# Halo columns by a matmul with the shifted identity, and a new instruction order, in the backward pass of a gated long-convolution block

## The chip, the cores and the metric

The kernel runs on one core of a Trainium2 chip. The metric is device time in microseconds (us), the median of several runs. One further execution is recorded by the hardware profiler; all profile lines come from it.

## The reference

The forward function takes a sequence of S = 2048 rows of D = 512 bfloat16 channels. With `xn = layernorm(q)` it computes

```python
k_shift = sum(k_pad[:, t:t+S, :] * shift_k[:, 3 - t] for t in range(4))  # 4 taps along the rows
kv = k_shift * v
y  = irfft(rfft(kv, 2S) * rfft(ssm_k, 2S))[:S] + kv * ssm_D               # long convolution along the rows
s  = xn * y
g  = silu((sigmoid(xn @ w_gate) * (xn @ w_up)) @ w_down)                  # F = 1376 hidden columns
out = q + s * g
```

The kernel must return `out` and, by `jax.vjp` with a given `grad_out`, the gradients of q, k, v, shift_k, ssm_k, ssm_D, w_gate, w_up and w_down: ten outputs. The change is in the part that computes the gradients of k and shift_k. Since `k_shift` at row r reads k at rows r-3 to r, the gradient of k at row r is a sum of four products, of `d(k_shift)` at rows r to r+3 with the four taps. `d(k_shift)` is `d(kv) * v`.

## The kernel before

**Layout.** The 2048 rows are laid out as 128 partitions by NJ = 16 consecutive rows (row = 16 p + j). The 512 channels are cut into NG = 4 column groups of GW = 128. All buffers in the core's own memory are views of one slab, so every row of the profile says `slab`. The long convolution is a Fourier transform done in steps by matmuls on TensorE, with evacuations from PSUM (the memory that matmuls write) by ACT or DVE between them, products on DVE, and transposes.

**Stages.** Generator functions ("streams") run side by side: the gated layer forward and the layer norm (`strG`, `ln`), the forward convolution (`strK`, `strX`, `strV`), the backward pass of the gated layer (`strZ`, `strD`), the weight gradients (`dW`, 33 sums of matmuls over the rows), and the convolution backward (`frontC`, `backC`). `backC` is the last stage, together with what is left of `dW`. It loops over the four column groups `cg`. In each one it multiplies spectra, transforms back (`inv2`, `inv1`), which gives `dkv`, and then fills a tile `dks` of 16 + 3 columns of 128 channels: columns 0 to 15 are `dkv * vg`, and columns 16 to 18, the halo, are the columns 0 to 2 of the next partition, because the row after the last one of partition p is the first one of partition p + 1. The last partition has no successor, so the halo is zeroed first from partition 96 on. Two transfers by SyncE (SP) then copy partitions 1 to 112 and 113 to 127 down by one. The readers of the halo are the multiplications of lag 1, 2 and 3 at the end of the group, `dks[:, lag:lag + 16]` by a tap, which DVE adds up into the gradient of k. The matmuls between them (the gradient of ssm_k from `B2`, and `pa`, the gradient of the taps, which reads `dks[:, 0:16]` alone) do not read the halo. In the last group the multiplications run in two halves of 8 columns, and `last_rows` turns the sums for shift_k and ssm_D by small matmuls, which an evacuation and a small store each follow.

**How the order is set.** No instruction is issued where the program text stands. A recorder (`Rec.add`) numbers every operation (6158 of them) with its reads and writes, and `Rec.emit` issues them all from one line, L505, so every row of the profile shows that line. A dictionary `ORDER` holds one list of operation numbers per engine (tensor, vector, scalar, gpsimd, sync): the fixed queue of that engine. `60+2` stands for 60, 61, 62. A sixth list, `moves`, gives the common order in which transfers are issued, whichever engine issues them. `nc.evac(dst, src, n)` records a copy that either ACT or DVE can do; the list in which its number stands decides. `BANKS` holds one digit per PSUM tile, which picks its bank among those its kind may use. Engines wait for each other where data or a buffer asks for it, by semaphores that the framework adds; a wait holds up all that stands behind it in that engine's queue.

**Names used below.** At the start: ACT's operation 69 is a small load of ssm_D (L860); 194 (cg 0) and 468 (a later group) are SP's transposing loads of ssm_k (`ld_KT`, L823); 505 is a load of q; 79 is SP's load of most of w_down (L867); 250, 251 and 252 are ACT's copies of broadcast taps from PSUM (L887); 327 and 307 are ACT's activations of the gated layer's first blocks (L761); 62 is a sine table for the transform (L576) and 112 a second one (L618); 222 and 223 are DVE's layer norm statistics (L716); 262 is the first evacuation of the forward convolution (L903). At the end: 5765 and 5766 are the last group's halo operations, 5921 to 5924 are DVE's copies in `last_rows` (L1441) and 5838 its copy of the sums for ssm_D (L1410), 5925 to 5931 the small matmuls that read them, 5979 to 6002 the multiplications and additions of lags 1 to 3 in the second half (L1432, L1434); 6022 to 6156 are matmuls and evacuations of `dW`, whose last sums have 256 and 96 columns; 5982, 6021, 6089, 6123 and 6157 are stores of `dW` in ACT's queue (L1322), and 5977 and 6019 SP's stores of the gradient of k.

Of the kernel before, what the change touches and what calls it, by code (L numbers as in the profile page):

```python
# [16 lines left out]
P = 128  # L17
# [6 lines left out]
NJ = 16  # L24
# [3 lines left out]
GW = D // NG  # L28
# [47 lines left out]
    """,  # L76
    "vector": """
# [552 lines left out]
def kernel_impl(ctx, tc, A_q, A_k, A_v, A_shift_k, A_ssm_k, A_ssm_D, B_x, B_w_gate, B_w_up, B_w_down,  # L630
                grad_out, out_0, out_1, out_2, out_3, out_4, out_5, out_6, out_7, out_8, out_9):
    nc = tc.nc
# [22 lines left out]
    def ps(kind, shape, dt=f32):  # L655
        return nc.ps(kind, shape, dt)

    ident = Ring(ar, [P]).ap
# [704 lines left out]
    def backC():  # L1363
        for cg in range(NG):
# [26 lines left out]
            dks = dks_r.next()  # L1391
# [20 lines left out]
            for j in range(NJ):  # L1412
                for s in range(4):
                    nc.tensor.matmul(pa[32 * s:32 * s + 32], dks[:, j, 32 * s:32 * s + 32], kh[:, j:j + 4, 32 * s:32 * s + 32],
                                     start=(j == 0), stop=(j == NJ - 1))
# [110 lines left out]
```

## Time and profile before

| quantity | value |
|---|---|
| median of 3 runs | 452.25 us (451.94 to 456.33) |
| profiled execution | 453.04 us, of which the span is 450.9 us |
| TensorE matmul (PE) | 435.4 us busy, 97%, 4868 instructions |
| TensorE weight load (PEld, beside PE) | 305.6 us, 68% |
| VectorE (DVE) | 408.5 us, 91%, 626 instructions |
| ScalarE (ACT) | 281.4 us, 62%, 351 instructions |
| GpSimd (POOL) | 23.8 us, 5% |
| mean granted TensorE clock | 0.989 |
| transfers | 117.24 MB, mean 260 GB/s |

The span runs from the first to the last recorded instruction; what lies around it (start and end of the program) is in the time and not in the span. Busy times are of one engine each, and engines run side by side. In the page's slices each digit is a fortieth of the span (11.3 us) and gives tenths; a 9 stands for 90% or more. In the groups, a row gives the output and input tiles, their shape and type, the count, and behind the bar the busy time, the mean in ns, and the idle time of the engine just before these instructions with what ended most of it. In the timeline, a row gives start and length in us, the engine, and in brackets the idle time before it and what ended that. The engine names with q (ACTq, SPq) are the same engines' issue of transfers.

### The profile page before, as it was taken

Reading aid. Unit: us, or ns where it says so; the run is one execution under the profiler, and the core shown is the slowest. Engines: PE = TensorE matmul, PEld = TensorE weight load, DVE = VectorE, ACT = ScalarE, POOL = GpSimd, SP = SyncE. Lnnn points to the kernel's source line nnn. Section 1 sums busy time; section 2 is a strip of 40 time slices with the busy share of each in tenths; the row PEclk is TensorE's granted clock in tenths of the full one; section 3 lists DMA queues with packets and bytes.
Section 4 is the critical chain, followed back from the end, with each engine's and each line's share of the span. In section 5 each row is a group of like instructions: output and inputs, shape, how many; then the busy total and the mean of one; then the engine's idle time right before and its main releaser. Section 6 shows DMA issues by size and latency. Waiting matters only on the chain.

```text
span 450.9 us, 11537 instructions
## 1 busy us (share of the span) xinstructions
PE 435.4 (97%) x4868; PEld 305.6 (68%) x4903; DVE 408.5 (91%) x626; ACT 281.4 (62%) x351; POOL 23.8 (5%) x46
## 2 busy tenths in 40 slices
PE   8799999999999999999999999999999999999993
PEld 4586686867767677565656754444577888887883
DVE  8689999999987899999999987789799999999983
ACT  7578998898687586475844253337477456565431
POOL 8210310010100000000000000000000000000000
PEclk9889999999999999999999999999999999999998
DMA  7987989878859799999999999999999999999998
GB/s 242 338 313 167 319 248 339 246 211 237 297 166 302 210 244 227 263 346 298 332 247 318 287 254 266 279 206 235 243 242 176 290 243 267 208 274 228 248 277 267
DMA packets 196701, 117.24 MB, mean 260 GB/s; under 512 B 107510, under 2 KB 183338, under 8 KB 196522
## 3 DMA queue, kind: packets, MB, share of 16 engines
q1 hardware_dynamic: 187496, 111.88, 94.8%
q10 hardware_dynamic: 9154, 4.62, 3.5%
q8 instruction: 38, 0.62, 0.5%
q14 instruction: 13, 0.11, 0.1%
HBM read 43.87 MB, written 46.70 MB: 201 GB/s over the span
## 4 chain that ended last, share of the span: by engine, by line
PE 85%; DMA 7%; DVE 2%; ACT 2%; issue 1%; SPq 1%; ACTq 0%; DVEq 0%
PE psum L505 85%; DMA slab<-in_A_ssm_k_dram 3%; DVE slab L505 2%; ACT slab L505 2%; DMA out_dram<-slab 2%; DMA slab<-slab 1%; DMA slab<-KD 1%; SPq L505 1%; ACTq L505 0%; DVEq L505 0%
## 5 line engine op out<-in xcount | busy, mean ns | idle before, releaser
L505 PE MATMUL psum<-slab 128*128 128x256 bf16 (+5 forms) x4868 | 435.4, 300 | 9.0 <-ACT slab L505 3.3
L505 PEld LDWEIGHTS <-slab 128*128 128x128 bf16 (+2 forms) x4903 | 305.6, 96 | 138.7 <-issue 33.0
L505 ACT CAST slab<-psum 128x1024 bf16<-128x1024 f32 (+2 forms) x220 | 189.5, 903 | 128.4 <-PE psum L505 111.4
L505 DVE TENSOR_TENSOR slab<-slab 128x1024 bf16<-128x1024 bf16 (+4 forms) x302 | 240.0, 833 | 6.6 <-ACT slab L505 3.0
L505 DVE STREAM_TRANSPOSE slab<-slab 128x1024 f32<-128x1024 f32 x48 | 64.9, 1360 | 8.2 <-ACT slab L505 5.0
L505 ACT ACTIVATE slab<-slab 128x512 bf16<-128x512 bf16 (+5 forms) x63 | 53.1, 875 | 23.8 <-DVE slab L505 23.7
L505 DVE CAST slab<-psum 128x1024 bf16<-128x1024 f32 (+2 forms) x29 | 32.1, 1111 | 6.4 <-PE psum L505 6.2
L505 DVE TENSOR_TENSOR slab<-psum,slab 128x512 bf16<-128x512 f32 (+2 forms) x52 | 31.6, 610 | 6.6 <-ACT slab L505 5.2
L505 ACT ACTIVATE slab<-psum 128x512 bf16<-128x512 f32 (+1 forms) x48 | 27.5, 575 | 8.5 <-DMA slab<-in_A_ssm_k_dram 4.3
L505 POOL MEMSET slab<- 128x128 bf16 (+3 forms) x10 | 4.5, 449 | 268.9 <-DVE slab L505 162.3
L505 POOL TENSOR_TENSOR slab<-slab 128x2 f32<-128x2 f32 (+3 forms) x11 | 12.1, 1106 | 89.3 <-DVE slab L505 89.2
L505 DVE SCALAR_TENSOR_TENSOR slab<-slab 128x2 f32<-128x2 f32 (+2 forms) x41 | 14.4, 360 | 0.3
L505 ACT ACT_TABLE_LOAD x10 | 12.8, 1283 | 1.9 <-PEq L1510 1.7
L505 DVE SCALAR_TENSOR_TENSOR slab<-psum,slab 128x512 bf16<-128x512 f32 x16 | 10.7, 684 | 1.9 <-PE psum L505 1.8
L505 DVE BATCH_NORM_STATS2 slab<-slab 128x6 f32<-128x512 bf16 x16 | 10.6, 681 | 0.4 <-DMA slab<-in_A_q_dram 0.4
L505 DVE STREAM_SHUFFLE slab<-slab 128x1024 f32<-128x1024 f32 x8 | 10.6, 1322 | 0.0
L505 ACT COPY slab<-psum 128x1024 bf16<-128x1024 bf16 (+2 forms) x10 | 7.9, 802 | 2.8 <-PE psum L505 2.8
L505 DVE TENSOR_SCALAR slab<-slab 128x512 bf16<-128x512 bf16 (+6 forms) x26 | 6.7, 274 | 0.7 <-POOL slab L505 0.5
L505 DVE COPY slab<-psum 128x512 bf16<-128x512 bf16 (+1 forms) x9 | 4.2, 507 | 2.2 <-PE psum L505 2.2
L505 POOL TENSOR_SCALAR slab<-slab 128x1 f32<-128x1 f32 (+3 forms) x10 | 4.5, 450 | 0.5
L505 DVE MEMSET slab<- 32x192 uint32 (+3 forms) x10 | 1.5, 160 | 1.3 <-PEq L1510 0.9
L505 DVE BATCH_NORM_AGGREGATE slab<-slab 128x2 f32<-128x6 f32 x16 | 2.5, 166 | 0.0
(13 smaller groups left out, 9.0 us busy)
## 6 DMA issues: line engine op xcount, KB each, us to landing
slab<-KD SPq DMA_DIRECT2D x16, 512.0 KB, 4.8
hD<-slab SPq DMA_DIRECT2D x8, 704.0 KB, 7.2
duD<-slab SPq DMA_DIRECT2D x8, 704.0 KB, 5.1
dgD<-slab SPq DMA_DIRECT2D x8, 704.0 KB, 4.3
slab<-in_A_k_dram SPq DMA_DIRECT2D x4, 1024.0 KB, 7.5
KD<-slab SPq DMA_DIRECT2D x8, 512.0 KB, 6.2
VD<-slab SPq DMA_DIRECT2D x8, 512.0 KB, 6.5
out_dram<-slab SPq DMA_DIRECT2D x16, 256.0 KB, 4.2
```

The lines of the kernel that those rows point to most:

```text
L505: getattr(getattr(self.nc, eng), meth)(*[place(v) for v in a], **{x: place(v) for x, v in k.items()})
```

## The change

In `backC` the two halo transfers of each group become one matmul and one evacuation. The weights of the matmul are the columns 1 to 127 of the identity, so that output partition m takes input partition m + 1; its moving data are `dks[:, 0:3]`, 384 columns. The result, 127 partitions by 3 x 128 in PSUM (kind "x", one bank), is then copied to `dks[0:127, 16:19]`.

```diff
             nc.vector.memset(dks[96:P, NJ:NJ + 3, :], 0.0)
-            nc.sync.dma_start(dks[0:112, NJ:NJ + 3, :], dks[1:113, 0:3, :])
-            nc.sync.dma_start(dks[112:127, NJ:NJ + 3, :], dks[113:128, 0:3, :])
+            ph = ps("x", [3, GW])
+            nc.tensor.matmul(ph[0:P - 1], ident[:, 1:P], dks[:, 0:3, :], start=True, stop=True)
+            nc.evac(dks[0:P - 1, NJ:NJ + 3, :], ph[0:P - 1], 384)
             nc.vector.tensor_tensor(dkv, dkv, ksh, ALU.mult)
```

Two operations take the place of two, so all other numbers stay. The pairs are 3895/3896, 4520/4521, 5168/5169 and 5765/5766 for the four groups: the first is now a matmul, the second an evacuation, on DVE in the first and last group (3896, 5766) and on ACT in the two others (4521, 5169). SP's list and `moves` lose these eight numbers. `BANKS` grows from 349 to 353 digits, and many others of its digits differ.

All six lists are in a new order, over the whole kernel. The start of the lists of vector, scalar and sync, and the ends of the lists of tensor, vector and scalar (the diff of the whole lists has 260 lines):

```diff
 "vector"
-        5 93+1 54+1 6 95+2 58+1 35 31 36 32 37 64 33 41+1 39+1 165 175 53 48 166 222 138 137 140 139 141 262 143 328
-        144+1 318 111 308 280 290 223 401 151 114 203 113 345 193 224 542 367 225 281 226 253 587 497 136 309 687 329
+        5 93+2 6 58+1 35+1 54 96 37 31+2 64 41 97 42 39 55 40 165 48 53 175 137 166 138 140 139 141 222+1 262 328 143
+        145 144 318 111 308 290 156 224 113 280 225 401 151 203 345 193 542 367 253 587 794 226 281 228 136 309 497
 "scalar"
-        1 68 60+2 66 65 67 249+1 327 69 307 252 3 251 279 112 156 192 410 438 541 363 362 586 596 560 135 477 524 686
+        1 68 60+1 66 65 67 249+1 69 327 251+1 307 3 279 112 62 192 410 438 541 363 362 586 596 560 135 477 524 686 385
 "sync"
-        0 75 4 74 76+1 73 43 70 78 72 71 194 83 82 84 2 80 146 79 468 85 505 231 118 232 440 330 344 364 331 851 916
+        0 4 75 73 76 70 43 74 77+1 72 71 194 83 82 2 84 468 505 146 79 231 85 80 364 118 440 344 232 330+1 851 365 708
...
 "tensor", last lines
-        5947+8 5960+14 5991+2 5916+3 5994+1 6022+18 5975 5920 6041+5 5839+63 6047+2 5996+2 6003+8 5769+15 6012+6
-        6050+3 6056+14 5802+15 6071+16 6124 6090+5 6125 6096+25 5925+3 5931 6126+29
+        5839+63 6009+3 6056 5769+15 6035 6057 5975 6013+5 6036+4 5765 6058+1 6041 5802+15 6042+11 6060+19 5925+3 5931
+        6090+5 6080+7 6096+25 6124+31
 "vector", last lines
-        5307+1 5934 5369 5935 5242 5658 5903+1 5921 5956+3 5976 5978+2 5922 5999 5923 6000 5924 6001+1 5838 5929
+        5369 5763 5307 5767 5935 5308 5978 5934 5658 5956+1 5242 5958 5903 5959 5904 5921 5976 5922 5764 5766 5923
+        5979+1 5999+1 5924 6001 5838 6002 5929
 "scalar", last lines
-        5676 5532 5709 5744 5605 5819 5936 5820 5981 5785 6054 5982 5937 6055 5818 6020 6088+1 6021 5932 6122+1 6156+1
+        5656 5742 5709 5605 5532 5744 5676 5819 5936 5785 5820 5981 5937 5982 6020+1 5818 6054 5932 6055 6088 6122
+        6089 6123 6156+1
```

More of the change, by code (lines that the diff above doesn't have):

```diff
@@ L33 @@
     "tensor": """
[42 rows of a table removed]
[44 rows of a table added]
     """,
     "vector": """
[24 rows of a table removed]
[25 rows of a table added]
     """,
     "scalar": """
[16 rows of a table removed]
[17 rows of a table added]
     """,
     "gpsimd": """
-        87 56+1 29 98+1 30 63 38 34 100 92 116 88 86 89 91 101 90 103+1 115 105 107 142 81 108+2 106 227 117 501 102
-        912 935 1326 1657 1929 2261 3541 4743
+        56 87 57 90 29+1 63 38 34 91 86 98 88 99 115 89 100 116 101 103+2 108 81 109 107 142 106 92 110 102 227 117
+        501 1326 935 912 1657 1929 2261 3541 4743
     """,
     "sync": """
[11 rows of a table removed]
[10 rows of a table added]
     """,
     "moves": """
[13 rows of a table removed]
[12 rows of a table added]
     """,
@@ L154 @@
 BANKS = (
-    "32012111000113121000231010100010000101110000101000011101011001001001232011100001100001013101011012010011001011"
-    "00001111101020110101010100100101010001100110101001101001100122032132101010330101011010110102110100011210103110"
-    "01011322211212202002100210310300011231102301100022211202020213011022331131022101010200201301110020331110301210"
-    "3100101012201301201"
+    "32200102131110310001321010100010000101110000101000011101011001001001231011100001100001013101011002011011001001"
+    "00001110101131110101010100100101010001100110101001101001100131032103101012300101121012010131101201011210023110"
+    "01011322211212100102101010310101001123110230110002122120220021301110200311310221010102102013011101120331210301"
+    "21031001012112201301213"
 )
```

196 rows, old and new, of the table ORDER are left out of this document.

## The prediction

> **What bounds the kernel now.** I read the page first: the span, the busy shares, the granted clock by slices, the chain that ended last.
>
> ```profile
> span 450.9 us, 11537 instructions
> PE 435.4 (97%) x4868; PEld 305.6 (68%) x4903; DVE 408.5 (91%) x626; ACT 281.4 (62%) x351; POOL 23.8 (5%) x46
> PEclk9889999999999999999999999999999999999998
> PE 85%; DMA 7%; DVE 2%; ACT 2%; issue 1%; SPq 1%; ACTq 0%; DVEq 0%
> ```
>
> TensorE is busy for 97% of the span, and 85% of the last chain is matmuls. DVE, at 91%, is close behind. The second and third digit of the clock are 8s: TensorE lost clock somewhere in the first 34 us. Next, busy time by stretches, for the middle and for the start:
>
> ```profile
> 25.00:150.00 125.00, 124.27 (x1516) 92.17 (x1526) 118.41 (x158) 105.89 (x137) 10.20 (x9) 1.00 0.81 253
> 150.00:300.00 150.00, 149.11 (x1045) 90.75 (x1061) 137.70 (x278) 79.53 (x95) 0.94 (x2) 1.00 1.06 273
> 300.00:440.00 140.00, 138.50 (x2087) 105.69 (x2092) 131.60 (x138) 77.82 (x96) 0.73 (x1) 1.00 1.09 245
> ...
> 14.70:15.80 1.10, 1.08 (x10) 0.82 (x9) 0.96 (x2) 0.00 (x0) 0.49 (x2) 1.00 1.11 352
> 15.80:18.10 2.30, 0.00 (x0) 0.00 (x0) 0.41 (x1) 1.03 (x2) 0.00 (x0) 1.00 1.14 306
> 18.10:19.00 0.90, 0.00 (x0) 0.00 (x0) 0.28 (x1) 0.64 (x3) 0.00 (x0) 0.50 1.09 277
> 19.00:24.90 5.90, 5.86 (x40) 4.80 (x40) 3.05 (x6) 4.55 (x6) 0.00 (x0) 0.50 1.05 337
> 24.90:28.00 3.10, 3.05 (x35) 2.67 (x34) 2.92 (x5) 2.35 (x3) 0.00 (x0) 0.99 0.54 137
> ```
>
> Columns: stretch, length, busy time of PE, PEld, DVE, ACT and POOL, granted clock, DMA share, GB/s. From 25 to 440 us TensorE idles 0.73 + 0.89 + 1.50 = 3.1 us in all, so no order can win more than that there. At the start it stands still from 15.8 to 19.0, and its clock is at half from 18.1 to 24.9. The timeline of that place (start, length, engine) and the chain name the cause:
>
> ```profile
> 12.37 0.38 ACT L505 ACTIVATE slab<-psum 128x256 bf16<-128x256 f32 x1
> 16.62 0.39 ACTq L505 DMA_DIRECT2D slab<-in_A_ssm_D_dram  x1
> 17.07 0.60 ACT L505 ACTIVATE slab<-psum 128x512 bf16<-128x512 f32 x1 [4.31 <-DMA slab<-in_A_ssm_k_dram]
> 19.04 2.29 PE L505 MATMUL psum<-slab 128*128 128x128 bf16 x16 [3.25 <-ACT slab L505]
> ...
> 7.55 9.06 DMA slab<-in_A_ssm_k_dram
> ```
>
> ACT's queue holds a small load of A_ssm_D (op 69, L860). It starts at 16.62, right after a load of A_ssm_k issued at 7.55 has landed (7.55 + 9.06 = 16.61). It reads nothing of that load; I infer that the two share one completion counter, and that the second user of a counter waits for the first. Behind op 69 stand ACT's evacuations (307, 252, 251), so ACT idles 4.31 us and TensorE, which waits for a PSUM bank, 3.25 us.
>
> **The halo transfers.** What they cost now, from the list of waits, the list of DMA issues, and the last group's timeline:
>
> ```profile
> DVE slab L505 <- DMA slab<-slab: 1.2, 1, 1.2
> ...
> slab<-slab SPq DMA_DIRECT2D x4, 84.0 KB
> slab<-slab SPq DMA_DIRECT2D x4, 11.2 KB, 5.2
> ...
> 425.86 0.66 SPq L505 DMA_DIRECT2D slab<-slab  x1
> 431.54 3.40 SPq L505 DMA_DIRECT2D slab<-slab  x1
> ...
> 438.33 1.42 DVE L505 TENSOR_TENSOR slab<-slab 128x1024 bf16<-128x1024 bf16 x2 [1.22 <-DMA slab<-slab]
> ```
>
> DVE waited once for a halo, 1.2 us, in the last of four groups; the other three are early enough. The eight transfers go (4 x 95 KB). SP is not idle without them: behind 425.86 stands a transposing load, which can start sooner.
>
> **What the change adds.** Four matmuls of 384 moving columns on the bound engine, four evacuations of 384 columns, two on ACT (4521, 5169) and two on DVE (3896, 5766).
>
> ```profile
> L505 PE MATMUL psum<-slab 128*128 128x256 bf16 x1696 | 203.3, 274 | 0.3 <-issue 0.2
> L505 PE MATMUL psum<-slab 128*128 128x512 bf16 x675 | 161.7, 382 | 3.4 <-DVE slab L505 1.2 <-issue 0.6
> L505 ACT CAST slab<-psum 128x384 bf16<-128x384 f32 x1 | 0.5, 499 | 0.0
> L505 DVE CAST slab<-psum 128x512 bf16<-128x512 f32 x5 | 3.3, 685 | 1.9 <-PE psum L505 1.9
> L505 DVE CAST slab<-psum 128x1024 bf16<-128x1024 f32 x23 | 28.1, 1222 | 4.5 <-PE psum L505 4.3
> L505 DVE BATCH_NORM_STATS2 slab<-slab 128x6 f32<-128x512 bf16 x16 | 10.6, 681 | 0.4 <-DMA slab<-in_A_q_dram 0.4
> L505 ACT ACT_TABLE_LOAD x10 | 12.8, 1283 | 1.9 <-PEq L1510 1.7
> L505 ACT ACTIVATE slab<-slab 128x1024 bf16<-128x1024 f32 x2 | 2.3, 1142 | 0.0
> ```
>
> Busy over count, 256 columns take 203.3 / 1696 = 0.12 us and 512 take 161.7 / 675 = 0.24. 384 lie midway: 0.18, four times **+0.7 us** (0.5 to 1.0). The ACT evacuations (0.50 each) lie in ACT's 38% of idle time. The DVE ones (under 0.69 each) are covered by DVE's 9%; without that cover they cost up to 1.4. The new matmul's readers: only DVE's multiplications of lag 1 to 3. TensorE holds behind each new matmul the weight-gradient matmuls; it waits for dks alone, written long before it in DVE's new order.
>
> [...]
>
> **The new order at the start.** ACT's list reads 250, 69, 327 where it read 250, 327, 69, and the loads before 69 are shuffled. Op 69 is now reached some 2 us sooner, when fewer loads have been issued ahead of it, so I expect it to follow an earlier user of its counter, one landed by about 12, in place of the A_ssm_k load. Then ACT goes on at 12.4 as before, 251, 252 and 307 are done before TensorE needs their banks, and the 3.25 us go. The half clock goes too: 5.86 us of matmuls at 0.50 would take 2.93, another 2.9 us. Together 6.15.
>
> What is late next: DVE now runs two more row statistics (222, 223, 0.68 each) ahead of evacuation 262, whose bank TensorE wants: I put the wait at 0.6. The sine table op 62 (1.14) moves behind op 112 and a table load (1.28), so the step that reads it waits, by counting ACT's work from 16.3 on, 0.5. Small ones, 0.4. Leaves 6.15 - 1.5 = **-4.6 us**, bounds 0 (op 69 still waits as long) and -6.15.
>
> [...]
>
> SP's list also changes there: the A_ssm_k load 468, which must wait for TensorE, now stands ahead of the w_down load 79.
>
> ```profile
> 19.18 0.43 SPq L505 DMA_DIRECT2D slab<-in_B_w_down_dram  x1
> ...
> 26.36 0.34 SPq L505 DMA_DIRECT2D slab<-in_A_ssm_k_dram  x1
> ...
> slab<-in_B_w_down_dram SPq DMA_DIRECT2D x1, 1280.0 KB, 7.6
> ...
> 36.74 2.29 PEld L505 LDWEIGHTS <-slab 128*128 128x128 bf16 x20 [0.23 <-issue]
> ```
>
> With the start 4.6 sooner, 468 goes at 21.8 and 79 some 1.4 later, after three issues of 0.34 to 0.43: 23.2 + 7.6 = 30.8. The last four of those twenty weight loads are the first that read w_down (from about 38.4; 33.8 then). Cover: 3 us.
>
> **The new order at the end.**
>
> ```profile
> 431.54 5.81 DMA slab<-slab
> 437.35 8.52 DMA out_dram<-slab
> ...
> 442.77 1.60 PE L505 MATMUL psum<-slab 128*4 128x128 bf16 x31 [0.44 <-DVE slab L505]
> 446.42 0.32 ACT L505 CAST slab<-psum 128x192 bf16<-128x192 f32 x1 [1.57 <-DMA out_dram<-slab]
> ...
> L505 PE MATMUL psum<-slab 128*128 128x96 bf16 x64 | 3.1, 206 | 0.0
> ```
>
> The last matmul ends at 442.77 + 1.60 = 444.37; the last evacuation starts 2.05 later, behind an output transfer, and 4.43 after that the span ends. In ACT's new list store 5982 stands ahead of the evacuations that held it, so those 2.05 can go. Against this, the small matmuls of last_rows move ahead of 64 matmuls of 96 columns and 8 of 256 (3.1 + 8 x 0.12 = 4.1 us before the end, where 30 of 96, 1.5, stood). They wait for DVE's copies. These are wanted 4.1 - 1.5 = 2.6 earlier and were 0.44 late already; DVE comes sooner by the 1.22 of the halo wait and one addition (6002, half width: 1.42 / 2 = 0.71) that moves behind the last of them (5838), less 0.5 for the halo copy, 1.4 in all; and TensorE is 0.7 later for its new matmuls. So they are 2.6 + 0.4 - 1.4 - 0.7 = 0.9 late, of which 0.4 is in the time already: +0.5. Of the 2.05 I take half, since a transfer's counter may still hold ACT once: 0.5 - 1.0 = **-0.5 us** (-2.0 to +1.6).
>
> **The middle.** Every engine's list is new, and no row prices that. Bounds: -3.1, its idle time; +3.25, the largest single TensorE wait of this trace. I take **+1.0**: more waits rather than fewer, since DVE gets a net of one evacuation more and 4.6 us less in which to hide, and the trace has single waits of TensorE of about a microsecond and less.
>
> Sum: 0.7 - 4.6 - 0.5 + 1.0 = -3.4. The profiled execution took 453.04 (span 450.9 and 2.1 around it): 449.6. The median of the runs is 452.25, 0.8 lower: **448.9**.
>
> **Rivals.**
> 1. The end comes out well and the middle free: TensorE finds the copies ready, the last evacuation follows the last matmul: 0.7 - 4.6 - 2.0 + 0 = -5.9, 446.4. For it: the 1.57 wait has no reason in the data it moves. Against: outputs of megabytes still drain there at full DMA share (1.09).
> 2. The lead is given back: DVE becomes the bound. It is busy 387.7 of 415 us between 25 and 440, and what TensorE gains at the start, DVE must gain too; a new order that queues it badly can cost 4 in place of 1: 0.7 - 4.6 - 0.5 + 4 = -0.4, 451.9. Against: DVE idled at the start as well (3.05 of 5.9 us busy), so it starts sooner.
> 3. Slower: op 69 still waits until 16.6. Now it stands ahead of 327 and a table load (1.28), so that the bank of the sixteen 256-column matmuls that ran before the stall is held too; they run after it: 16 x 0.12 = 1.9, at half clock 3.8. Say +3: 3 + 0.7 - 0.5 + 1.0 = +4.2, 456.4. It decides from the point at which the wait of op 69 ends later than about 13.
> That the halo matmul by itself does nothing for the time is part of the forecast: its worth is +0.7 against a 1.2 wait of DVE, not of TensorE.
>
> **Chances.** Forecast 0.50, first rival 0.20, second 0.22, third 0.08. A measurement of this kernel tells about 1% (4.5 us) from no change. Faster by more (under 447.7): most of the first rival and a little of the forecast, 0.25. Slower by more (over 456.8): half of the third, 0.04. Within: 0.71. The range runs from 446.0, a first rival with a little of the bounds below it, to 453.0, the second with some of the middle's bound.
>
> **What would show it.** Right: op 69's row before 12.5, no TensorE wait over 1 us before 30, clock 1.00 from 4.5 on, the 25 us stretch reached 4 to 5 us sooner; 4872 matmuls in the count or near it, no slab to slab rows among the plain transfers; a TensorE wait for DVE about 4 us before its end; the last evacuation within 1 us of the last matmul. Wrong: the clock's 8s still there, a w_down row as what ends a TensorE wait near 34, or waits in 25 to 440 adding up to more than 5 us.

## The result and the profile after

| | before | after |
|---|---|---|
| median, 8 runs each | 451.98 us (448.99 to 456.33) | 446.66 us (445.85 to 448.17) |
| profiled execution (span) | 453.04 (450.9) | 445.85 (443.7) |

The ratio is 0.989, 95% interval 0.987 to 0.992: about 5 us faster. The forecast was 448.9, the range 446.0 to 453.0. The two profiled executions lie further apart (7.2 in the span) than the medians (5.3), because that of before is 1.1 above its median and that of after 0.8 below. A few executions of e5 (498.96 to 1145.13 us), e6 (2531.81) and e9 (801.97) took far longer than the rest, one of e5 with a profile at a granted clock of 0.75; the medians below are of the others, and e5 was profiled again.

The page of after, its span, busy shares, clock by slices and chain:

```profile
span 443.7 us, 11573 instructions
PE 435.5 (98%) x4907; PEld 303.8 (68%) x4907; DVE 409.3 (92%) x629; ACT 279.8 (63%) x352; POOL 20.9 (5%) x46
PEclk9999999999999999999999999999999999999999
PE 88%; DVE 6%; ACT 2%; DMA 1%; POOL 1%; issue 1%
```

The two 8s of the clock are gone, and of the DMA's 7% of the chain 1% is left. Busy time by stretches of after (columns as in the prediction):

```profile
14.70:19.00 4.30, 4.30 (x52) 3.98 (x50) 4.28 (x10) 3.49 (x5) 0.00 (x0) 1.00 0.93 259
19.00:24.90 5.90, 5.77 (x75) 4.72 (x74) 5.39 (x9) 5.85 (x8) 0.00 (x0) 1.00 0.83 261
25.00:150.00 125.00, 124.27 (x1511) 89.74 (x1509) 117.45 (x157) 102.36 (x133) 7.37 (x9) 1.00 0.83 264
150.00:300.00 150.00, 150.00 (x1046) 91.28 (x1044) 138.88 (x278) 79.79 (x97) 0.73 (x1) 1.00 1.05 276
300.00:440.00 140.00, 139.35 (x2138) 106.96 (x2135) 130.69 (x141) 77.87 (x99) 0.73 (x1) 1.00 1.10 252
```

From 19.0 to 24.9 TensorE now does 75 matmuls where it did 40, at full clock. The timeline of after, the two loads in ACT's queue, the first waits of TensorE, and the end:

```profile
10.89 0.40 ACTq L507 DMA_DIRECT2D slab<-in_A_ssm_D_dram  x1
13.92 0.37 ACTq L507 DMA_DIRECT2D slab<-in_B_w_up_dram  x1
...
8.25 23.76 PE L507 MATMUL psum<-slab 128*128 128x128 bf16 x283 [1.25 <-DVE slab L507]
...
438.83 0.67 PE L507 MATMUL psum<-slab 128*128 128x96 bf16 x12
439.55 0.32 ACT L507 CAST slab<-psum 128x192 bf16<-128x192 f32 x1 [1.04 <-PE psum L507]
439.89 0.38 ACTq L507 DMA_DIRECT2D out_dram<-slab  x1
```

The last evacuation follows the last matmul (438.83 + 0.67 = 439.50) by 0.05 us where it followed by 2.05.

To see where time comes from and goes, one table serves all runs. Each matmul has a weight load (4907 of each in after), and the loads' starts follow each other in TensorE's list. The time from a load's start to the next one's, summed over the matmuls that ran in a given stretch of before, less the same sum in before, gives what that work gained (-) or lost. Where nothing changes, these sums mostly agree within a few hundredths; e10 has an exception of 1.5, told there.

| us against before | 0-25 | 25-60 | 60-330 | 330-440 | last 4.3 | halo | last matmul's end | from there to the span's end |
|---|---|---|---|---|---|---|---|---|
| before | | | | | | | 444.37 | 6.48 |
| after | -5.15 | +1.57 | -0.27 | -0.58 | -0.73 | +0.28 | 439.51 | 4.18 |
| e1_69early | -1.26 | 0.00 | 0.00 | +1.36 | +0.30 | | 444.78 | 6.56 |
| e2_start_new | -5.24 | +1.39 | +0.47 | +1.23 | +0.29 | | 442.53 | 6.55 |
| e3_tail_new | -2.94 | 0.00 | +0.04 | +8.31 | -0.73 | | 449.07 | 3.39 |
| e4_halo_only | -1.77 | +0.01 | 0.00 | +0.46 | -0.60 | +0.54 | 443.02 | 6.21 |
| e5_again | -5.95 | +0.02 | +0.17 | +0.80 | +0.79 | | 440.20 | 6.37 |
| e6_new_dma | -5.32 | +1.57 | -0.39 | +20.21 | -0.73 | | 459.73 | 3.64 |
| e7_late_loads | -4.85 | +1.22 | -0.28 | +0.74 | -0.73 | +0.32 | 440.81 | 6.24 |
| e8_halo_x9 | -5.78 | +1.58 | -0.28 | -0.77 | -0.73 | +5.53 | 443.93 | 3.02 |
| e9_old_start | -5.44 | +0.01 | -0.08 | -0.21 | -0.73 | +0.28 | 438.20 | 6.26 |
| e9b_old_start24 | -5.45 | +2.53 | -0.28 | +0.04 | -0.73 | +0.33 | 440.83 | 6.11 |
| e10_tail_mm | -3.39 | 0.00 | +0.24 | +1.89 | -0.34 | +0.54 | 443.32 | 6.19 |

### The profile page after: what moved, and what is told of

Read it like the earlier page. It is cut to its first block, busy times and chain, and to the rows that moved or that the text cites. A ratio compares the mean times of both kernels' runs of the same rounds, so it can differ in the third digit from the quotient of the medians.

```text
span 443.7 us, 11573 instructions
## 1 busy us (share of the span) xinstructions
PE 435.5 (98%) x4907; PEld 303.8 (68%) x4907; DVE 409.3 (92%) x629; ACT 279.8 (63%) x352; POOL 20.9 (5%) x46
## 4 chain that ended last, share of the span: by engine, by line
PE 88%; DVE 6%; ACT 2%; DMA 1%; POOL 1%; issue 1%
PE psum L507 88%; DVE slab L507 6%; ACT slab L507 2%; POOL slab L507 1%; DMA slab<-in_A_q_dram 1%; DMA slab<-in_A_ssm_k_dram 1%
## 5 line engine op out<-in xcount | busy, mean ns | idle before, releaser
L507 ACT CAST slab<-psum 128x1024 bf16<-128x1024 f32 (+5 forms) x224 | 190.4, 892 | 119.5 <-PE psum L507 96.0
L507 ACT ACTIVATE slab<-slab 128x512 bf16<-128x512 bf16 (+5 forms) x61 | 50.9, 875 | 30.8 <-DVE slab L507 30.7
L507 DVE CAST slab<-psum 128x1024 bf16<-128x1024 f32 (+3 forms) x29 | 32.6, 1131 | 5.1 <-PE psum L507 4.3
L507 POOL TENSOR_TENSOR slab<-slab 128x2 f32<-128x2 f32 (+3 forms) x11 | 11.0, 1000 | 97.3 <-DVE slab L507 97.2
L507 POOL TENSOR_SCALAR slab<-slab 128x1 f32<-128x1 f32 (+3 forms) x10 | 3.3, 335 | 0.4
```

The lines of the kernel that those rows point to most:

```text
L507: getattr(getattr(self.nc, eng), meth)(*[place(v) for v in a], **{x: place(v) for x, v in k.items()})
```

## The experiments

Times are medians as said above; ratios are to before in the same session, with 95% intervals.

**e1: the load of ssm_D alone.**

```diff
 "scalar"
-  ... 249+1 327 69 307 252 3 251 ...
+  ... 249+1 69 327 307 252 3 251 ...
```

> Before, with one edit: in ACT's list the small load of ssm_D (69) stands ahead of the activation 327 instead of behind it; nothing else moves. Theory start (the load's wait for an earlier transfer holds ACT, then TensorE, then the clock): the wait of TensorE of 3.25 us at 15.8 goes, the granted clock stays 1.00 in the second and third slice, the half-clock loss of 2.5 us goes: -5.7, about 446.3. Theory DVE (the lead is given back, since DVE must gain it too): the start is 5 us sooner, TensorE's idle time after 25 us grows from 3.1 to 5 or more, time 450 or above. Theory counter wrong (the load waits for the ssm_k load itself): it still starts at 16.6, time 452 or more.

452.48 us, ratio 1.001 (0.999 to 1.004): nothing. The timeline of e1:

```profile
10.39 0.40 ACTq L508 DMA_DIRECT2D slab<-in_A_ssm_D_dram  x1
...
17.87 0.42 ACTq L508 DMA_DIRECT2D slab<-in_B_w_up_dram  x1
18.33 0.58 ACT L508 CAST slab<-psum 128x512 bf16<-128x512 f32 x1 [4.60 <-DMA slab<-in_A_k_dram]
...
18.96 1.27 PE L508 MATMUL psum<-slab 128*128 128x128 bf16 x16 [3.18 <-ACT slab L508]
```

The load of ssm_D no longer waits (10.39), so the inference of the shared counter holds here. The semaphores recorded in the traces agree: in before this load and load 194 are on one (108), which 194 raised by landing at 16.60, and the load left at 16.62; in e1 it waits on that of load 70, which had been issued at 4.55. But ACT is idle all the same, 4.60 us, and what ends that is a load of k (83), whose counter the second load in ACT's list, w_up (3), waits for until 17.87 (in before both are on semaphore 109: 83 landed at 17.96, and w_up left at 17.99). Behind it stands evacuation 251. Before has the same wait hidden behind the first:

```profile
17.99 0.38 ACTq L505 DMA_DIRECT2D slab<-in_B_w_up_dram  x1
```

Two loads held ACT one after the other, and the prediction saw the first.

**e2: the new start in front of the old order.** S is the set of operations that had started by 60 us in before, closed under what they depend on; halo by transfers.

```diff
-  list = before's list
+  list = [n in after's list if n in S] + [n in before's list if n not in S]
```

> Before, with the new order (all six lists and banks) for the operations that ran in the first 60 us, the old order behind them, halo transfers as before. Theory start: TensorE's work of the first 60 us ends about 3.6 to 5 sooner (3.4 for the wait, 2.5 for the clock, against a new wait of 1.25 near 7.0), time 447 to 448.4, no better than the edit of the load alone. Rival (the rest of the new start is worth something too): 445.5 or below. Theory DVE: 450 or above.

450.07 us, ratio 0.996 (0.994 to 0.998). The start wins 5.24 and loses 1.39 behind 25 us; of the 3.85 left, 2.0 are lost in the old order behind it (0.47 + 1.23 + 0.29), in waits of TensorE: from 25 us on the list of waits has 2.3 for DVE (1.2 in before) and one of 0.8 whose end the profile puts down to nothing (issue). The largest, in the timeline of e2 (before has 0.76 and 0.44 in the places of the last two):

```profile
337.59 61.38 PE L508 MATMUL psum<-slab 128*32 128x128 bf16 x957 [0.84 <-issue]
...
400.47 39.81 PE L508 MATMUL psum<-slab 32*32 32x512 bf16 x618 [0.85 <-DVE slab L508]
440.93 1.60 PE L508 MATMUL psum<-slab 128*4 128x128 bf16 x31 [0.65 <-DVE slab L508]
```

Between the start's theory and DVE's: each is half right.

**e3: the new end behind the old order**, halo by transfers. S is what had started by 410 us, in before's order; the rest is in after's order.

```diff
-  list = before's list
+  list = [n in before's list if n in S] + [n in after's list if n not in S]
```

> Before, with the new order for what ran after 410 us (halo still by transfers, the memset of the last group's halo back ahead of them). Theory tail (order of ACT's stores and of the small matmuls of the last rows): the last evacuation follows the last matmul within 1 us instead of 2.05, TensorE's wait of 0.44 goes: -2 to -3, about 449.5. Rival (the end is bound by what is still to be written out): within 0.7 of before, 451.3 to 452.7.

456.36 us, ratio 1.010 (1.007 to 1.013): slower, which neither expected. The seam brought a wait of its own:

```profile
419.52 0.62 PE L508 MATMUL psum<-slab 32*32 32x512 bf16 x8 [5.30 <-DVE slab L508]
...
419.50:423.80 4.30, 3.78 (x43) 1.82 (x43) 4.26 (x4) 2.64 (x4) 0.00 (x0) 0.50 1.10 201
```

DVE's new list takes the third group's multiplications sooner than its halo transfers land, and TensorE stands behind DVE; after the pause its clock is at 0.50 in all of the second row. The last evacuation does start 0.04 after the last matmul, but the stores had the time of the pause to drain. As a test of the end the run is lost; it says that this part of the new order and the transfers, at these places, don't go together.

**e4: the code edit alone**, in the old order: eight transfers out, four matmuls and evacuations (all on ACT) in, at the first place where dks is ready and a bank free.

```diff
 "tensor"
+  3895 ahead of 3898, 4520 ahead of 5062, 5168 ahead of 5608, 5765 ahead of 5991
 "scalar"
+  3896 ahead of 4159, 4521 ahead of 5188, 5169 ahead of 5604, 5766 ahead of 5936
```

> Before, with the code edit alone: halo by matmul and evacuation, put into the old order where dks is ready and a bank is free, the evacuations on ACT. Theory start and tail (the matmul is worth nothing by itself): four matmuls of 0.07 to 0.18 us, DVE's wait of 1.2 gone, TensorE as before: 451.5 to 452.7. Rival halo (DVE's late halo and the eight transfers among the stores matter): 451 or below, with the last rows' matmuls of TensorE no longer waiting and the final stores landing sooner.

452.21 us, ratio 1.000 (0.997 to 1.003): the matmul by itself is worth nothing. DVE's wait for the halo is gone and the last rows' matmuls gain 0.60, against 0.54 of new matmuls.

**e5: both loads.**

```diff
 "scalar"
-  ... 249+1 327 69 307 252 3 251 279 112 ...
+  ... 249+1 69 327 307 252 251 279 112 3 ...
```

> Before, with two edits in ACT's list: the load of ssm_D (69) ahead of 327 as in the last run, and the load of w_up (3) behind 251, 279 and 112 instead of ahead of 251. The first run showed that moving 69 alone leaves TensorE's wait (3.18 us at 15.78), with 3 then the load that holds ACT until 17.87. Theory two loads: the wait goes and the clock stays 1.00, TensorE's first 25 us take 5.0 to 5.5 less; behind it DVE's lag takes back some 1.5 to 3 as in the second run (0.85 at the first group's pa matmuls, 0.4 and 0.3 later): 448.5 to 450.5. Rival DVE alone (the whole start is given back): 451.5 or more. Rival start (nothing is given back): 447 or less.

448.53 us, ratio 0.992 (0.990 to 0.995): most of after's gain, by two numbers of one list. For the profile it was run again:

> The fifth kernel again, for a profile at full clock (the first one was taken at 0.75). Theory two loads: no wait of TensorE above 0.5 us between 6 and 30, clock 1.00 there, ACT's load of ssm_D at 10.4; waits of TensorE for DVE of about 0.85 near 337 and 0.4 to 0.9 near 400 show the lead given back. Rival: no such waits, the span 445 or less.

```profile
10.67 0.39 ACTq L508 DMA_DIRECT2D slab<-in_A_ssm_D_dram  x1
17.28 0.38 ACTq L508 DMA_DIRECT2D slab<-in_B_w_up_dram  x1
...
10.21 9.98 PE L508 MATMUL psum<-slab 128*128 128x256 bf16 x110 [0.16 <-issue]
...
396.39 0.41 PE L508 MATMUL psum<-slab 32*32 32x512 bf16 x8 [0.40 <-DVE slab L508]
397.64 37.80 PE L508 MATMUL psum<-slab 32*32 32x512 bf16 x581 [0.85 <-DVE slab L508]
435.73 0.54 PE L508 MATMUL psum<-slab 128*128 128x96 bf16 x9 [0.28 <-ACT slab L508]
437.06 3.15 PE L508 MATMUL psum<-slab 128*128 128x96 bf16 x59 [0.79 <-DMA slab<-duD]
```

TensorE runs from 10.21 without a stop, and the start wins 5.95, more than the whole new start does. The old order then gives 1.8 back; the wait of 0.85 is no part of that, since before has 0.76 in the same place. The wait near 337 came out at 0.25, not 0.85. So the time came out in the expected range, but not for the reason expected: TensorE's waits for DVE from 25 us on are 1.3 in all, where before has 1.2. What is new are 0.79 for a transposing load and 0.28 for ACT, and the rest is small.

**e6: the new order without the matmul.**

```diff
-            ph = ps("x", [3, GW])
-            nc.tensor.matmul(ph[0:P - 1], ident[:, 1:P], dks[:, 0:3, :], start=True, stop=True)
-            nc.evac(dks[0:P - 1, NJ:NJ + 3, :], ph[0:P - 1], 384)
+            nc.sync.dma_start(dks[0:112, NJ:NJ + 3, :], dks[1:113, 0:3, :])
+            nc.sync.dma_start(dks[112:127, NJ:NJ + 3, :], dks[113:128, 0:3, :])
```

> After, with the halo by the two transfers again (put back into SP's list next to the same neighbours, the last group's memset back ahead of them): the new order without the matmul. Theory (the matmul matters only as what lets the new order run, since multiplications of lag 1 to 3 now follow dks within a few us): DVE waits 4 to 10 us for transfers in the groups 2 to 4, TensorE behind it 4 to 6, time 450.5 to 454. Rival (the matmul is worth nothing): 446 to 447.5.

465.42 us, ratio 1.031 (1.027 to 1.035): 19 slower than after, beyond both. The list of waits, the timeline and two stretches of e6:

```profile
DVE slab L509 <- DMA slab<-in_A_k_dram: 9.3, 1, 9.3
DVE slab L509 <- DMA slab<-slab: 6.8, 1, 6.8
...
381.37 30.65 PE L509 MATMUL psum<-slab 32*32 32x512 bf16 x506 [7.00 <-DVE slab L509]
421.73 3.54 PE L509 MATMUL psum<-slab 32*32 32x512 bf16 x35 [9.71 <-DVE slab L509]
...
411.61 3.99 SPq L509 DMA_DIRECT2D slab<-slab  x1
...
381.37:386.08 4.71, 4.71 (x42) 2.85 (x42) 4.47 (x4) 2.94 (x3) 0.00 (x0) 0.50 1.19 232
421.73:427.04 5.31, 5.31 (x45) 3.23 (x45) 5.31 (x5) 1.93 (x2) 0.00 (x0) 0.50 0.00 0
```

Both are waits for the halo. The second row names a load of k, which landed at 419.01; but the waiting multiplication (5344, at 419.31) reads nothing of it, only the third group's halo, whose second transfer (5169) landed at 419.22. SP reaches that transfer at 411.61, three others behind the first half (407.54), and its issue then takes 3.99, although the earlier user of its counter had landed at 407.27; what draws the issue out is not shown. So the halo comes 9 to 12 us after dks. In the third group of after, matmul and evacuation take 1.3 (398.81 to 400.07):

```profile
398.68 1.39 ACT L507 CAST slab<-psum 128x1024 bf16<-128x1024 f32 x2 [0.28 <-PE psum L507]
398.81 2.51 PE L507 MATMUL psum<-slab 128*127 128x384 bf16 x33 [0.16 <-DVE slab L507]
```

Not all of the 20.8 us by which TensorE falls behind after between 330 and 440 (20.21 + 0.58) is waiting: the two pauses are 16.7, and behind each the clock is at 0.50, for 10.0 us of matmuls in all (last two rows of e6), which takes most of the rest. Other places for the transfers might cost less; the run shows what they cost at these.

**e7: the old sequence in ACT's list, the other loads as in after.**

```diff
 "scalar"
-  ... 249+1 69 327 251+1 307 3 279 112 62 192 ...
+  ... 249+1 327 69 307 252 3 251 279 112 62 192 ...
```

> After, with ACT's list in the old sequence at that place: 327, 69, 307, 252, 3, 251. By the compiled program the two loads still follow early users of their counters (78 and 72, which landed at 12.5 and 13.9 in the profile of after), since the other loads keep the new order. Theory counter (what counts is which earlier transfer the load must wait for): 69 starts near 12.6 and 3 near 14, TensorE waits under 1 us, 446.5 to 448. Rival list (what counts is the place in ACT's list): the 3 us wait and half clock return, 449.5 to 452.

447.32 us, ratio 0.991 (0.988 to 0.994). The timeline of e7:

```profile
13.26 0.39 ACTq L508 DMA_DIRECT2D slab<-in_A_ssm_D_dram  x1
...
13.75 0.44 ACTq L508 DMA_DIRECT2D slab<-in_B_w_up_dram  x1
```

The loads stand behind the same operations as in before, and leave at 13.26 and 13.75 where they left at 16.62 and 17.99. The earlier users of their counters, 78 and 72 by the expectation, had landed at 12.54 and 13.90 in after. So the place in ACT's list alone does not bring the stall; in these runs it came where an earlier user of the counter landed late.

**e8: the matmul nine times.**

```diff
+                for _ in range(9 if op.n in (3895, 4520, 5168, 5765) else 1):
                     getattr(getattr(self.nc, eng), meth)(...)
```

> After, with each of the four halo matmuls issued nine times in a row (the same result): 32 matmuls of 384 columns more. By the row estimate of 0.18 each +5.8, by the times between matmul starts in the old order (0.54 for four) 0.135 each +4.3, by those of after (0.28 for four) 0.07 each +2.2. Rival (TensorE has room there, DVE being the bound): +1 or less.

449.66 us, 3.0 above after's median. In TensorE's list the 32 more cost 5.53 - 0.28 = 5.25, 0.164 each; the row of the group gives 0.18, so the row's price is the nearest of the three:

```profile
L509 PE MATMUL psum<-slab 128*127 128x384 bf16 x36 | 6.6, 327 | 0.2 <-DVE slab L509 0.2
```

Against the profile of after, the last matmul ends 4.4 later, but the span only 3.3: from there to the end it takes 3.02 in place of 4.18, probably because the stores had longer to drain.

**e9 and e9b: the old start, with both loads moved, in front of the new order and its matmuls.** As in e2 with the two orders exchanged, S up to 60 us (e9) and up to 24 us (e9b).

```diff
-  list = after's list
+  list = [n in e5's list if n in S] + [n in after's list if n not in S]
```

> After, with the operations that ran in the first 60 us in the old order, but with both loads moved in ACT's list as in the fifth run; the new order and the halo matmul from there on. The new start has a wait of TensorE of 1.25 us at 7.0 and its matmuls between 25 and 60 us take 1.57 longer in sum than in the old order. Theory (these 2.5 are the price of the new start, and the rest of the new order keeps what is won): 444.0 to 445.5. Rival (DVE takes it back, as it did behind the old order): 446 to 447.5.

445.21 us, ratio 0.984 (0.980 to 0.988), as the theory expected and the lowest of all, though its interval overlaps that of after (0.987 to 0.992). TensorE ends 1.31 sooner than in after. The 1.57 is saved; the wait of 1.25 is not there, but waits of 0.64 at 5.54 and 0.49 at 18.36 are, so the first 25 us win only 0.29 more. Against before the new order gives nothing back. Its profiled execution, though, took 446.6:

```profile
435.83 2.37 PE L508 MATMUL psum<-slab 128*128 128x96 bf16 x52
437.86 0.38 ACTq L508 DMA_DIRECT2D out_dram<-slab  x1
438.33 0.81 ACT L508 CAST slab<-psum 128x512 bf16<-128x512 f32 x2 [3.54 <-PE psum L508]
439.93 0.32 ACT L508 CAST slab<-psum 128x192 bf16<-128x192 f32 x1 [0.79 <-ACT slab L508]
```

Store 6055 in ACT's list leaves at 437.86, when SP's large store 4741, on the same counter (semaphore 100 for both in after), has landed (437.78); three evacuations stand behind it. So the last one starts 1.73 after the last matmul (2.05 in before), with after's own lists.

> As the run with the old order in the first 60 us, but with the old order only for what ran in the first 24 us. Theory: it saves the wait of 1.25 at 7.0, not the 1.57 behind 25 us: 445.0 to 446.2. Rival (DVE takes it back): 446 to 447.5.

449.65 us, ratio 0.994 (0.991 to 0.997): a miss. The seam brought new waits between 25 and 60 us (+2.53).

**e10: the new end behind the old order, with matmuls.** As e3, on e4's kernel, from 420 us.

> The halo by matmul in the old order (the fourth run), with the new order for what ran after 420 us: the end alone, this time with matmuls. Theory tail (the counters that ACT's last stores wait for are free sooner, since SP's large stores go out 4 to 7 us earlier, and the last evacuation no longer stands behind such a store): the last evacuation ends within 0.5 us of the last matmul instead of 2.1, the span ends 4.2 after it instead of 6.2: 449.5 to 450.5. Rival (the end is bound by what is still to be written out): 451.5 to 452.5.

451.45 us, ratio 0.996 (0.993 to 0.999). The rival is nearer. The end of e10:

```profile
443.05 0.38 ACTq L508 DMA_DIRECT2D out_dram<-slab  x1
443.52 0.81 ACT L508 CAST slab<-psum 128x512 bf16<-128x512 f32 x2 [3.61 <-PE psum L508]
445.08 0.32 ACT L508 CAST slab<-psum 128x192 bf16<-128x192 f32 x1 [0.75 <-ACT slab L508]
```

Here 4741 was issued at 433.48 (427.80 in after) and landed at 442.97; 6055 followed at 443.05, and the last evacuation ended 2.08 after the last matmul, as in e4 (2.11). The order of ACT's last stores decides nothing by itself; when SP's large stores get out does. The +1.89 in the table says little of the new end: 1.50 of it is a wait of TensorE at 373.52, where all lists are still those of e4, which has no such wait there. One execution of the same order can differ that much from another.

## Why the prediction was right or wrong

The direction and the range held, the range at its lower end, 0.66 above it. Two terms of four were off by 1.9 and 2.5 us in the same direction, and the range held because it had been drawn to reach the first rival. By the terms of the sum, with the two profiled executions (-7.2 in all; that of after is the fastest of its eight):

- **Halo matmuls, +0.7.** 0.28 between starts of loads in after, 0.54 in e4, 4 x 0.164 = 0.66 by e8: right by e8 and e4, and below its bound of 0.5 in after itself. DVE's halo wait went, and that was worth nothing to TensorE (e4), as stated.
- **Start, -4.6.** -5.15 up to 25 us and +1.57 from there to 60: -3.6. The size was near, the cause half named. "Op 69 still waits" was taken as the one point on which the start hangs; e1 shows that 69 alone wins none of the 3.25, because op 3 held ACT to 17.87, and e5 that both together win it all. The new list happened to move both, and the step passed over the second. It could have been read off ACT's list, `252 3 251`, and the row of before at 17.99. That the term came out near is in part luck. "What is late next" was put at 1.5 in three small waits; it was one wait of 1.25 for DVE at 7.0 (ahead of the layer norm's matmuls, not at evacuation 262, and against the sign "no TensorE wait over 1 us before 30"), and 1.57 of slower sequences behind 25 us, which no step foresaw and whose cause is not shown. The load of w_down, by contrast, went as worked out: issued at 22.59 and landed at 31.25, where 23.2 and 30.8 were forecast.
- **Middle, +1.0.** -0.27 and -0.58: -0.85. This step failed in its sign. What the second rival says, that the lead is given back, exists: behind the old order 2.0 of 3.9 are lost (e2), 1.8 of 5.9 (e5), and all of e1's 1.26. That it goes through DVE holds in e2 and e1 (waits for DVE of 2.3 and 2.2 from 25 us on, against 1.2) and not in e5 (1.3). Behind the new order nothing is lost in after and e9, and TensorE's idle time from 25 to 440 us fell from 3.1 to 1.4; in e7, with the same lists there, one wait of 0.88 for a transposing load near 425 accounts for its +0.74. What in the new order keeps the middle free, among thousands of moves, was not taken apart.
- **End, -0.5.** -0.73 for the last matmuls, which found DVE's copies ready ("0.9 late" was wrong, and the wait announced for 4 us before the end is not there), and 6.48 - 4.18 = 2.30 behind the last matmul: -3.0 in this execution. The bound of -2.05 for the last evacuation was taken in full where half was counted. But it is no fixed gain: e7 and e9 have the same lists at the end, and there the last evacuation starts 1.69 and 1.73 behind again.

So the first rival's time (446.4, "the end comes out well and the middle free") is nearer to the median of 446.66 than the forecast of 448.9, and its two conditions are the two that the profile of after meets. The third rival fell with op 69's row at 10.89.

The value of the code edit itself lies in none of these terms. Alone it is worth nothing (e4), and the new order with the transfers in its place is 19 us slower (e6, at the places tried): with the matmul the halo is there 1.3 us after its data, and the order may put the multiplications right behind. The start's gain does not need it (e5).

What stays open: when SP's stores near the end get out. In the four runs in which the last evacuation follows the last matmul at once, the transposing load 5938 held SP for 2.36 (after), 1.27 (e3 and e6) and 1.32 (e8); in e9 it held it for 5.59 and in e7 for 6.03, and all later stores follow. No run separates whether the lists before it or the load on the transfers decide that. It may differ between executions of one kernel: those of e9 lie at 445.1 to 445.2 and at 446.6 to 447.1, the profiled one among the latter. With one profile of each kernel this is not shown.

## What to carry to other kernels

A small transfer in the list of an engine that also evacuates PSUM can be a hidden wait: one of ACT's left here at 16.62, when an earlier transfer on its counter had landed at 16.60, and ACT idled 4.31 us. Look up which earlier transfer shares the counter and when that one lands, and do it for every transfer that the engine issues there, since taking away the first wait may only show the next (17.87 in e1). A sum of gains at the start is worth what the lists behind it let through: look at which engine or transfer the bound waits for next (DVE in e2, a transposing load in e5), and not only at busy shares. When a transfer is replaced by something quicker, the gain may come only with an order that uses it, so try the edit and the order apart and together.

## What the runs showed of the hardware

The half clock lasted 6.8 us in before and 3.41 in e1 and e4, and did not follow every pause. In before TensorE paused 3.25 us from 15.79, and the clock was at 0.50 from 18.1 to 24.93, 6.8 us. In e1, with a pause of 3.18 from 15.78, it fell at 20.13, when TensorE was already at work again, and for 3.41 us. In e4, with 2.66 from 15.79, it fell from 18.77 to 22.18. In e3, with 2.85 from 15.79, and in e10, with 2.32 from 15.86, it did not fall. So the length of the pause alone does not tell these runs apart: with 2.66 the clock fell, with 2.85 it did not. Stretches of e1, of e4 and of e3:

```profile
20.10:20.20 0.10, 0.10 (x3) 0.06 (x1) 0.10 (x2) 0.10 (x1) 0.00 (x0) 0.64 1.00 302
20.20:23.40 3.20, 3.20 (x21) 2.51 (x19) 1.83 (x4) 3.16 (x5) 0.00 (x0) 0.50 1.06 330
23.50:23.60 0.10, 0.10 (x5) 0.10 (x3) 0.10 (x1) 0.03 (x1) 0.00 (x0) 0.80 1.08 369
```

```profile
18.70:18.80 0.10, 0.10 (x6) 0.10 (x4) 0.00 (x0) 0.10 (x1) 0.00 (x0) 0.84 0.54 93
18.80:22.10 3.30, 3.30 (x22) 2.55 (x20) 2.58 (x4) 3.25 (x5) 0.00 (x0) 0.50 1.03 321
22.10:22.20 0.10, 0.10 (x3) 0.04 (x2) 0.00 (x0) 0.10 (x1) 0.00 (x0) 0.59 1.12 399
```

```profile
18.60:25.00 6.40, 6.22 (x73) 5.50 (x72) 5.63 (x10) 6.34 (x9) 0.00 (x0) 1.00 1.09 342
```

By the table's first stretch, less what the pause itself was shorter, half clock costs 2.5 us in before (e3 wins 2.94, of which 0.40 is pause) and 1.35 in e1 and e4, which win 1.2 of the 2.5. That may be why the profile of before stands a little above its median.

Behind the longer pauses, 5.30 in e3 and 7.00 and 9.71 in e6, the clock is at 0.50 at least for the 4.30, 4.71 and 5.31 us of the rows shown there. What decides whether the clock falls, and for how long, was not shown. The same pause can cost more or less: 3.25 us in before came with 2.5 of half clock, 3.18 in e1 with 1.35.

In the trace of before 286 transfers of SP and ACT raise eight semaphores, so all but the first eight have an earlier user of the same one ahead of them. For 138 of these the trace tells when that user landed, and none was issued sooner; in after it tells it for 202 of 270, and none was issued sooner there either. The two need not move the same data: in before ACT's load of 128 x 3 values left at 16.62, when one of 512 KB on the same semaphore had landed at 16.60. A change in the order of the loads changes which transfer that is: in after the same load follows one of shift_k, issued at 4.66, and leaves at 10.89, and w_up (3) leaves at 13.92, when an earlier load of w_up has landed at 13.90. At the end of e9 three evacuations stand behind a store that left at 437.86, 0.08 after one of SP had landed. The transfer that the list of waits names need not be the one waited for: in e6 it names a load of k, which landed at 419.01, where the multiplication at 419.31 reads the halo, which landed at 419.22.
